# Two softmaxes of each item moved ahead of ScalarE's PSUM copies: a fused top-k attention and GELU MLP on one core

## The chip, the cores and the metric

The kernel runs on one core of a Trainium2 chip. The metric is the device time of one execution in microseconds (us). Five engines work side by side, each through its own list of instructions in order, and they wait for each other through semaphores: TensorE (PE; PEld is its weight load), VectorE (DVE), ScalarE (ACT), GpSimd (POOL) and SyncE (SP), which here only issues DMA transfers. Matrix products land in PSUM, where each named buffer ("bank") must be copied out before it can be written again.

## The reference

```python
scores = scale * np.matmul(q, k.transpose(0, 1, 3, 2))        # q, k, v: (8, 8, 576, 64)
kth = np.partition(scores, -top_k, axis=-1)[..., -top_k:-top_k + 1]   # top_k = 32
scores = np.where(scores >= kth, scores, -1000000000.0)
attn = np.exp(scores - np.max(scores, axis=-1, keepdims=True))
attn = attn / (np.sum(attn, axis=-1, keepdims=True) + 1e-09)
x = np.matmul(attn, v)              # -> (4608, 512), heads side by side
h = x @ w_in                        # (512, 2048)
g = 0.5 * h * (1.0 + erf(h / sqrt(2)))
return g @ w_out                    # (2048, 512)
```

Everything is float32.

## The kernel before

**Items and slots.** Attention is cut into 144 *items*. An item is 128 query rows of a pair of heads of one batch, so it has two score rows of 576 keys per partition (e = 0 and 1). A batch has 18 items: 16 main ones and two *last* ones (they hold the rows 512 to 575 of two pairs; `t == NM` in the code). Even batches have their last items at the end, odd batches at the start, so that four last items stand together: 52 to 55, 88 to 91, 124 to 127 (and 16 to 19 near the start). The loop at line 1174 runs over *slots* n = 0 to 147. In slot n different items are at different stages; the code writes each engine's instructions in the order in which that engine will take them:

- `scores(n + 2)`, and in even slots `scores(n + 3)` too: PE multiplies queries by keys (L406; L421 for a last item), ACT copies the result out of PSUM (L414, L425). Last items get their scores in slots of their own, odd ones included (items 53 and 55 in slots 51 and 53).
- `attend(n - 3)`: for an odd item PE makes `o` from the finished probabilities `pt` and the values (L727; L738 for last items), and `copy_x()` has ACT copy it into `xT` (L732, L744). Last items are attended later (`mids`, `even_last`): 52 in slot 56, 53 in slot 57, 54 and 55 in slot 59.
- `mlp(...)`: pieces of the MLP for tokens that are done, on PE. In even slots these are products with `w_in` (L790 into `h_ps`), in odd slots first the last such piece, then products with `w_out` (L944 into `seven`, L946 into `y_ps`). In odd slots `run_gelus()` (L806) follows the last `h_ps` piece, and ACT copies `seven` out (L962, L965).
- `transposes(n - 2)`: probabilities turned over for `attend`, by PE in odd slots (`tails`: `tp_t` L371 or L385 and L647, copied by L379 or L390 and L650; `both`: `tp` L661, copied by L676). For even items DVE transposes blocks (L595) and SP writes them to DRAM and reads them back (`write_p` L605, `read_p` L615); there only the small `t_ps` is left for PE (L371, copied by L379).
- `softmax(n - 1, e)` on ACT: `select` (L536, a Prelu with slope 2^100 that drives all scores below the k-th far down, needs `neg`) and then the exponential (L548, needs `bias`, and adds the row up into `den`; a short read of the accumulator follows).
- `top_k(n)` on DVE: four rounds of eight maxima and their replacement (L502, L505). Its last act is `inverse(n - 1)`, the reciprocal of `den` (L523). Then POOL makes `neg` and `bias` (`threshold(n)`, L516, L517), multiplies item n - 1 by the reciprocal (`normalise`, L571) and adds halves of later rows (`sum_up`, L466; `smaller`, L474). `add_small(n - 1)` (L529) stands on POOL behind `smaller(n + 1)` and before `threshold(n)`, and the reciprocal waits for it.

So there is a ring from slot to slot: end of top-k on DVE, threshold on POOL, two softmaxes on ACT, `add_small` on POOL, reciprocal on DVE at the end of the next top-k.

**PSUM.** From slot 13 on (`few[0]`, n > START + 2 with START = 10) the small results `o`, `seven`, `t_ps` and `tp_t` share one bank, tag "z": each needs the copy of the one before. `tp` and one of the two score tiles share the pair "pr", the other score tile and `h_ps` the pair "l1".

**ACT's order before,** in slots from 13 on: scores' copies; `copy_x`; in odd slots the gelus; the copy of `seven`; softmax(n - 1, 0); the copies of `tails` and `both` (or of `t_ps`); softmax(n - 1, 1); then in odd slots the remaining copies. The gelus and the exponentials need different function tables, so ACT loads a table (1.28 us) before the gelus and again before the first exponential that follows.

Of the kernel before, what the change touches and what calls it, by code (L numbers as in the profile page):

```python
# [14 lines left out]
def kernel(  # L15
# [83 lines left out]
    def issue_soon():  # L99
        while soon:  # L100
            soon.pop()()
# [140 lines left out]
    def waits(u):  # L242

        return u == ORDER[-1]
# [3 lines left out]
    def weights_add(u):  # L248
        if u in words:
            w, _, _, d = parts(u)  # L250
            nc.gpsimd.tensor_tensor(d, d, w.bitcast(i32), op=ALU.add)
        made.add(u)
# [22 lines left out]
    few = [False]  # L275
# [75 lines left out]
    def row(i, e):  # L351
        return S_of[i][:, e * S : (e + 1) * S]
# [178 lines left out]
    def select(i, e):  # L531

        if i < 0 or i >= N:
            return
        st, s = stat_of[i], row(i, e)
        nc.scalar.activation(s, s, func=AF.Prelu, bias=st["neg"][:, e : e + 1], scale=1.0, alpha=STEEP)  # L536
        selected.add((i, e))
# [3 lines left out]
    def softmax(i, e):  # L541

        if i < 0 or i >= N:
            return
        st, s = stat_of[i], row(i, e)
        if (i, e) not in selected:
            select(i, e)
        nc.scalar.activation(  # L548
            s, s, func=AF.Exp, bias=st["bias"][:, e : e + 1], scale=1.0,
            accum_out=st["den"][:, e : e + 1],  # L550
        )
# [23 lines left out]
    def squared(i):  # L575

        if not SINGLE.stop - 2 < i < N - 2:
            return False
        return items[i][1] == NM or (i % 2 == 0 and i % RINGS != 12)

    def delayed(i):

        return squared(i) and items[i][1] == NM
# [23 lines left out]
    def read_p(i):  # L607

        if squared(i):
            d = turned.pop(i)  # L610
            if i % 2 == 0:
                pt_now[0] = pt_tile()
            cols = slice(i % 2 * P, (i % 2 + 1) * P)
            for k in range(P // SQ):
                nc.sync.dma_start(  # L615
                    out=pt_now[0][k * SQ : (k + 1) * SQ, :, cols], in_=d[:, :, k, :]
                )
# [70 lines left out]
    def closes(i):  # L688

        if not few[0] or i < 0 or i >= N:  # L690
            return False
        pair, t = items[i]
        return t < NM and t % 2 == 1 and pair % NP == NP - 1

    def copy_x():
        while copies:
            copies.pop()()
# [369 lines left out]
    def run_gelus():  # L1067
        while waiting:
            gelus(waiting.pop(0))
            if eager[0]:  # L1070
                run_small(9)

    def run_small(room):

        while summing:
            sums(summing.pop(0))
            room -= 4
        while small and room > 0:
            n, f = small.pop(0)
            f()  # L1080
            room -= n
# [11 lines left out]
    def mlp(n):  # L1093
        for _ in range(n):
            if done[0] >= len(pieces) or pieces[done[0]][0] > ready[0] or left[0] == 0:
                return
            pieces[done[0]][1]()
            done[0] += 1
            left[0] -= 1
            if eager[0]:  # L1100
                run_gelus()
                run_small(9)
# [8 lines left out]
    def room_in(n):  # L1111

        x = n - START - 1
        if x < 1:
            return 4
        if x >= len(sizes):
            return 0
        return sizes[x] + (1 if x % 2 == 0 else -1) + 2 * (bare(n) - bare(n + 1))
# [55 lines left out]
    for n in range(ahead):  # L1174

        held[0] = n < N and squared(n - 2)
        mid = [i for i in (n - 5, n - 4) if delayed(i) and n % 2 and (i % 2 or i in starts)]
        even_last = delayed(n - 4) and n % 2 == 0 and n - 4 not in starts
        if not mid and not even_last:
            read_p(n - 3)  # L1180

        def mids():
            attend(mid.pop(0))
            if not mid:
                copy_x()
                read_p(n - 3)
                issue_soon()
        left[0] = room_in(n)
        few[0] = n > START + 2
        eager[0] = n > N  # L1190
        left[0] += closes(n - 3) - closes(n - 2)
        if not waits(unit_in(n)):
            weights_add(unit_in(n))
        if n > 0:
            larger(n + 1)
        for piece in squares_in.pop(n, []):
            piece()
        if n == 1:

            for e in range(2):  # L1200
                select(0, e)
            for e in range(2):
                softmax(0, e)
        two = few[0] and n % 2 == 0 and n + 3 < N and items[n + 3][1] < NM
        scores(n + 2, two)
        if two:
            scores(n + 3)
        if even_last:
            product = attend(n - 4)
            issue_soon()  # L1210
            read_p(n - 3)
        else:
            product = not delayed(n - 3) and attend(n - 3)
        if len(mid) == 2:
            mids()
        late = n > START
        if n != 1 and n < START:

            for e in range(2):
                select(n - 1, e)  # L1220
            softmax(n - 1, 0)
        copy_x()
        if n == START:

            for e in range(2):
                select(n - 1, e)
            softmax(n - 1, 0)
        if waits(unit_in(n)):
            weights_size(unit_in(n))
            weights_add(unit_in(n))  # L1230
        mlp(1)
        if closes(n - 3):
            ready[0] = n_tok[0]
        if few[0] and n % 2:
            run_gelus()
        tr = transposes(n - 2)
        if product and n > START and done[0] < len(pieces) and pieces[done[0]][0] > ready[0]:

            for piece in tr[:1]:
                piece(n + 2 if few[0] else None)  # L1240
            tr, ready[0] = tr[1:], n_tok[0]
        if not few[0] and n > START:
            softmax(n - 1, 0)
        mlp(1)
        if n != 1 and not late:
            softmax(n - 1, 1)
        if few[0]:
            softmax(n - 1, 0)
            if n % 2:
                mlp(ODD)  # L1250
                if mid:
                    mids()
        mlp(1)
        prep = prep_in.pop(n, [])
        if n == 0:
            weights_size(unit_in(1))
            keep_busy(14, ident)
        if n == START + 1:

            for piece in prep:  # L1260
                piece(None)
            prep = []
        if len(prep) > 1 and len(tr) == 3:
            tr, prep = tr[:1] + prep[:1] + tr[1:], prep[1:]
        now = tr[:-1]
        if few[0]:
            now, tr, prep = tr + prep[:1], [], prep[1:]
        for x, piece in enumerate(now):
            piece(n + 2 if few[0] else None)
            ready[0] = n_tok[0]  # L1270
            if few[0] and x == 2:
                break
            mlp(1)
        ready[0] = n_tok[0]
        if late:
            softmax(n - 1, 1)
        if n > 0:
            smaller(n + 1)
        add_small(n - 1)
        for piece in tr[-1:] + prep:  # L1280
            piece(None)
            mlp(1)
        if n < START:

            keep_busy(4 if n == 0 else 8 if product else 14 if n < 5 else 18, ident)

        run_gelus()
        mlp(left[0])
        run_gelus()
        if n < N:  # L1290
            top_k(n, lambda: inverse(n - 1), lambda: square_p(n - 2))
            write_p(n - 2)
            flush()
            if n == 0:
                larger(1)
        else:
            inverse(n - 1)
        threshold(n)
        if n == 0:
            smaller(1)  # L1300
        normalise(n - 1)
        sum_up(n + 2)
        if n in sums_in:
            weight_sums(sums_in[n])
        run_small(6)

        if n > 0 and not waits(unit_in(n + 1)):
            weights_size(unit_in(n + 1))
        run_stores()
        if n == N:  # L1310
            run_stores()
        for m in (n + 1, n + 2):

            if m > 2 and waits(unit_in(m)) == (m == n + 1):
                load_weights(m)
        if n < NP:
            load("v", n)
        if n == 5:
            nc.vector.memset(flat["k"][0][TL:, 0:TL], 0.0)
            load("q", SQUARES)  # L1320
            load("k", SQUARES)
# [38 lines left out]
```

## Time and profile before

| | |
|---|---|
| median of 3 runs | 1477.53 us (1476.33 to 1479.15) |
| the profiled execution | 1479.29 us, of which span 1477.5 us |
| instructions | 26521 |
| TensorE's granted clock | 0.999 |
| ACT in the whole span | 1082.8 us busy (73%) |
| POOL | 1142.0 us (77%) |
| L536 select | 288, mean 788 ns |
| L548 exponential | 288, mean 782 ns, and 288 reads of 194 ns |
| table loads for L806 and for L548 | 68 and 67, 1283 ns each |

In the timelines a row has the start in us, the length in us, the engine, the line in the code, the operation, the tiles as out<-in, shapes, how many instructions were merged into the row, and in brackets how long the engine stood idle before it and what ended that. Rows of merged PE instructions end with the last one's modelled end. In the list of waits a row has who waited for whom, the sum in us, how many times, and the longest. In the table by stretches the busy time of each engine follows the stretch's bounds and length.

### The profile page before, as it was taken

Reading aid. Unit: us, or ns where it says so; the run is one execution under the profiler, and the core shown is the slowest. Engines: PE = TensorE matmul, PEld = TensorE weight load, DVE = VectorE, ACT = ScalarE, POOL = GpSimd, SP = SyncE. Lnnn points to the kernel's source line nnn. Section 1 sums busy time; section 2 is a strip of 40 time slices with the busy share of each in tenths; the row PEclk is TensorE's granted clock in tenths of the full one; section 3 lists DMA queues with packets and bytes.
Section 4 is the critical chain, followed back from the end, with each engine's and each line's share of the span. In section 5 each row is a group of like instructions: output and inputs, shape, how many; then the busy total and the mean of one; then the engine's idle time right before and its main releaser. Section 6 shows DMA issues by size and latency. Waiting matters only on the chain. (4 is left out here: it accounts for less than half of the span.)

```text
span 1477.5 us, 26521 instructions
## 1 busy us (share of the span) xinstructions
PE 1449.7 (98%) x8693; PEld 1134.6 (77%) x8693; DVE 1307.8 (89%) x3331; ACT 1082.8 (73%) x1902; POOL 1142.0 (77%) x1290
## 2 busy tenths in 40 slices
PE   8999999999999998999999999999999999999999
PEld 6776677887777776888777777787777777787787
DVE  7999899999999999899999999899999999898701
ACT  7999877877777686777777777677777777677620
POOL 6877567878898888777898978787788888887632
PEclk9999999999999999999999999999999999999999
DMA  7425210045435356345534347344543435523300
GB/s 198 144 86 129 78 47 1 24 92 103 93 71 91 67 107 129 65 95 112 102 81 78 74 74 151 76 92 96 99 101 73 89 63 97 125 61 73 68 15 15
DMA packets 544713, 127.04 MB, mean 86 GB/s; under 512 B 466464, under 2 KB 536128, under 8 KB 544576
## 3 DMA queue, kind: packets, MB, share of 16 engines
q1 hardware_dynamic: 543312, 124.93, 39.8%
q8 instruction: 69, 1.13, 0.3%
q14 instruction: 68, 0.56, 0.1%
q10 hardware_dynamic: 1200, 0.39, 0.1%
q0 software_dynamic: 64, 0.03, 0.0%
HBM read 80.47 MB, written 44.83 MB: 85 GB/s over the span
## 5 line engine op out<-in xcount | busy, mean ns | idle before, releaser
L790 PE MATMUL h_ps<-xT,w_in_sb 128*128 128x256 f32 (+1 forms) x2560 | 534.1, 361 | 0.0
L790 PEld LDWEIGHTS h_ps<-xT,w_in_sb 128*128 128x128 f32 x2560 | 437.5, 190 | 73.3 <-issue 25.2
L502 DVE MAX8 top<-lists 128x8 f32<-128x576 f32 (+1 forms) x792 | 475.5, 639 | 0.0
L505 DVE MATCH_REPLACE8 lists<-top,lists 128x288 f32<-128x288 f32 (+1 forms) x528 | 307.6, 588 | 0.0
L571 POOL TENSOR_TENSOR s<-s,stat 128x1152 f32<-128x1152 f32 x135 | 286.1, 2119 | 0.3 <-DVE stat L523 0.3
L536 ACT ACTIVATE s<-s,stat 128x576 f32<-128x576 f32 x288 | 224.7, 788 | 16.6 <-POOL stat L516 16.4
L548 ACT ACTIVATE s<-s,stat 128x576 f32<-128x576 f32 x288 | 224.6, 782 | 11.3 <-POOL lists L466 0.7
L529 POOL TENSOR_SCALAR stat<-stat 128x2 f32<-128x2 f32 x144 | 31.6, 219 | 210.4 <-ACT s L548 183.8
L474 POOL TENSOR_TENSOR lists<-lists 128x576 int32<-128x576 int32 x132 | 186.4, 1412 | 4.0
L466 POOL TENSOR_TENSOR lists<-s 128x576 int32<-128x576 int32 x133 | 188.0, 1413 | 0.0
L727 PE MATMUL o<-pt,raw_v 128*64 128x256 f32 x1280 | 152.9, 384 | 4.3 <-DMA pt<-turned 2.4
L806 ACT ACTIVATE g<-h_ps 128x512 f32<-128x512 f32 x144 | 78.2, 594 | 107.0 <-PE h_ps L790 106.8
L727 PEld LDWEIGHTS o<-pt,raw_v 128*64 128x64 f32 x1280 | 87.9, 136 | 88.3 <-issue 43.1
L946 PE MATMUL y_ps<-w_out_sb,sum 128*128 128x256 f32 x472 | 140.8, 380 | 0.0
L414 ACT ACTIVATE s<-s_ps 128x1024 f32<-128x1024 f32 x127 | 124.9, 1031 | 9.2 <-PE s_ps L406 8.8
L406 PE MATMUL s_ps<-kt,qm 64*128 64x512 f32 x512 | 129.4, 618 | 0.8 <-ACT s L412 0.8
L676 ACT COPY pt<-tp 128x1024 f32<-128x1024 f32 x73 | 74.4, 1019 | 56.2 <-PE tp L661 56.1
L505 DVE MATCH_REPLACE8 lists<-first,lists 128x288 f32<-128x288 f32 x264 | 114.2, 438 | 0.0
L946 PE MATMUL y_ps<-w_out_sb,g 128*128 128x256 f32 x480 | 113.4, 379 | 0.0
L523 DVE RECIPROCAL stat<-stat 128x2 f32<-128x2 f32 x144 | 22.9, 159 | 95.2 <-POOL stat L529 94.4
L502 DVE MAX8 first<-lists 128x8 f32<-128x288 f32 x268 | 106.5, 436 | 0.0
L441 DVE TENSOR_TENSOR lists<-s 128x576 f32<-128x576 f32 x133 | 101.1, 760 | 0.0
(162 smaller groups left out, 2483.3 us busy)
## 6 DMA issues: line engine op xcount, KB each, us to landing
turned<-s SPq DMA_DIRECT2D x240, 144.0 KB, 3.5
pt<-turned SPq DMA_DIRECT2D x240, 144.0 KB, 3.2
raw_v<-in_v_dram SPq DMA_DIRECT2D x64, 128.0 KB, 3.0
raw_q<-in_q_dram SPq DMA_DIRECT2D x112, 72.0 KB, 2.3
raw_k<-in_k_dram SPq DMA_DIRECT2D x112, 72.0 KB, 2.4
out_dram<-y SPq DMA_DIRECT2D x30, 256.0 KB, 2.1
w_out_sb<-in_moe_w_in_dram SPq DMA_DIRECT2D x14, 511.8 KB, 4.8
w_out_sb<-in_moe_w_out_dram SPq DMA_DIRECT2D x10, 511.8 KB, 4.1
```

Of the source, the lines that this page charges most:

```text
L406: nc.tensor.matmul(s_ps[:, e], lhsT=q_t[rows, :], rhs=kt[rows, main_keys(pair)], start=True, stop=True)
L414: nc.scalar.activation(spread(s, S + TL, SM), s_ps, func=AF.Copy, scale=scale)
L466: nc.gpsimd.tensor_tensor(t[:, :, 1].bitcast(i32), a.bitcast(i32), b.bitcast(i32), op=ALU.add)
L474: nc.gpsimd.tensor_tensor(into_of(i)[:, :, 1].bitcast(i32), both, top, op=ALU.subtract)
L502: nc.vector.max(x[:, e], src[:, e])
L505: nc.vector.match_replace(dst[:, e], x[:, e], src[:, e], LOWEST)
L536: nc.scalar.activation(s, s, func=AF.Prelu, bias=st["neg"][:, e : e + 1], scale=1.0, alpha=STEEP)
L548: nc.scalar.activation(s, s, func=AF.Exp, bias=st["bias"][:, e : e + 1], scale=1.0, accum_out=st["den"][:, e : e + 1],)
L571: nc.gpsimd.tensor_tensor(s, s, wide, op=ALU.mult)
L727: nc.tensor.matmul(o[e * D : (e + 1) * D, 0:n], lhsT=vt[:, j, e, :], rhs=pt[:, e * NJ + j if j < NM else NM, :], start=(j == 0), stop=(j = ...
L790: nc.tensor.matmul(h_tile(u)[:, i, :], lhsT=w_in_sb[:, ko, f * P : (f + 1) * P], rhs=xT[:, ko, c0 : c0 + n], start=(ko == 0), stop=(ko == ...
L946: nc.tensor.matmul(acc[names][:, k], lhsT=lhsT, rhs=rhs, start=(j == 0 and k == 0), stop=(j == FT // 2 - 1 and k == 1),)
```

## The change

In slots from 13 on ACT's order is changed and nothing else; PE, DVE, POOL and SP get the same instructions in the same order.

- Odd slots: both selects stand ahead of `copy_x`, the gelus and the copy of `seven`; both exponentials stand where softmax(n - 1, 0) stood, ahead of the copies of `tails` and `both`, and ahead of a `copy_x` that `mids` calls.
- Even slots: select 0, exponential 0 and select 1 stand ahead of `copy_x`, exponential 1 right behind it.
- Nothing is left behind the copies of the turned probabilities.

```diff
         if n != 1 and n < START:
             for e in range(2):
                 select(n - 1, e)
             softmax(n - 1, 0)
+        if few[0]:
+            select(n - 1, 0)
+            if n % 2 == 0:
+                softmax(n - 1, 0)
+            select(n - 1, 1)
         copy_x()
+        if few[0] and n % 2 == 0:
+            softmax(n - 1, 1)
         if n == START:
...
         if n != 1 and not late:
             softmax(n - 1, 1)
         if few[0]:
-            softmax(n - 1, 0)
             if n % 2:
+                softmax(n - 1, 0)
+                softmax(n - 1, 1)
                 mlp(ODD)
                 if mid:
                     mids()
...
         ready[0] = n_tok[0]
-        if late:
+        if late and not few[0]:
             softmax(n - 1, 1)
```

`softmax` calls `select` only where it has not been called for that item and row.

## Prediction

> **What bounds the kernel now.** I read the engines' busy times on the profile's first part, then the stretches of 200 us, then the list of waits.
>
> ```profile
> PE 1449.7 (98%) x8693; PEld 1134.6 (77%) x8693; DVE 1307.8 (89%) x3331; ACT 1082.8 (73%) x1902; POOL 1142.0 (77%) x1290
> ...
> 1100.00:1300.00 200.00, 196.74 (x1188) 152.68 (x1186) 186.35 (x477) 145.91 (x259) 167.96 (x190) 0.99 0.44 92
> ...
> POOL stat L529 <- ACT s L548: 183.8, 71, 6.0
> ...
> DVE stat L523 <- POOL stat L529: 94.4, 91, 9.8
> ...
> PE o L738 <- DMA pt<-turned: 5.7, 3, 2.2
> ...
> PE o L727 <- DMA pt<-turned: 2.4, 2, 1.9
> ...
> ACT s L536 <- POOL stat L516: 16.4, 12, 2.7
> ```
>
> PE is the bound: 27.8 us of the span are not its own, and in a late stretch it works 196.74 of 200 us. Its list does not change, so a gain can only come out of its waits; the rows with `pt` hold 8.1 us, most of what there is in the slots that the change touches. DVE has 13.65 us of 200 to spare, and 94.4 us in all go to the reciprocal that waits for `add_small`, which waits 183.8 us for the exponentials. So earlier softmaxes let DVE and POOL run ahead of PE, but PE does not need them earlier in most slots. What matters is whether ACT, now waiting for the threshold ahead of its copies, makes PE wait.
>
> **An ordinary pair of slots**, 44 (even) and 45 (odd), from the timeline:
>
> ```profile
> 429.26 1.94 ACT L414 ACTIVATE s<-s_ps 128x1024 f32<-128x1024 f32 x2 [0.21 <-PE s_ps L406]
> ...
> 429.44 0.22 POOL L516 TENSOR_SCALAR stat<-top 128x2 f32<-128x2 f32 x1
> ...
> 432.43 0.37 ACT L732 COPY xT<-o 128x256 f32<-128x256 f32 x1 [1.23 <-PE o L727]
> ...
> 435.01 0.38 PE L371 MATMUL t_ps<-kt,qm 128*128 128x128 f32 x2
> ...
> 435.60 0.77 ACT L536 ACTIVATE s<-s,stat 128x576 f32<-128x576 f32 x1
> ...
> 436.40 0.78 ACT L548 ACTIVATE s<-s,stat 128x576 f32<-128x576 f32 x1
> ...
> 437.08 0.19 ACT L548 ACTIVATION_READ_ACCUMULATOR s<-s,stat 128x1 f32 x1
> ...
> 439.03 0.22 POOL L516 TENSOR_SCALAR stat<-top 128x2 f32<-128x2 f32 x1
> ...
> 439.75 1.09 ACT L806 ACTIVATE g<-h_ps 128x512 f32<-128x512 f32 x2 [1.18 <-PE h_ps L790]
> ...
> 440.72 0.38 ACT L965 COPY p<-seven 128x256 f32<-128x256 f32 x1
> ...
> 441.84 1.28 ACT L548 ACT_TABLE_LOAD   x1
> ...
> 443.00 0.38 PE L371 MATMUL tp_t<-kt,qm 128*128 128x128 f32 x2
> ...
> 443.13 0.78 ACT L548 ACTIVATE s<-s,stat 128x576 f32<-128x576 f32 x1
> ...
> 447.67 0.19 ACT L548 ACTIVATION_READ_ACCUMULATOR s<-s,stat 128x1 f32 x1
> ```
>
> A select costs 0.80 (435.60 to 436.40), an exponential with its read 0.87 (436.40 to 437.27).
>
> *Even slot.* The scores' copy ends at 431.20; `neg` was there at 429.66. Select, exponential, select take 2.47, where ACT now idles 1.23 for PE. `copy_x` then ends at 431.20 + 2.47 + 0.37 = 434.04 instead of 432.80. The next user of bank z is `t_ps` at 435.01. The 1.24 us lie inside a slack of 2.21: cost 0. Without that cover it would cost 1.24 per pair of slots.
>
> *Odd slot.* `seven`'s copy ends at 441.10, the next user of z, `tp_t`, starts at 443.00: slack 1.90. If `neg` is early, the two selects (1.60) lie in the idle time before the gelus, and only the order changes: behind `seven`'s copy (next start 440.97) come the table 1.28 and two exponentials 1.74, so both softmaxes are done at 444.0 and not 447.86, and the copy of `tp_t` begins about where it did. If `neg` is late, everything hangs behind it: from `neg` to the end of `seven`'s copy it is 1.60 + 1.28 + 0.97 (gelus to L965's start) + 0.38 = 4.2. With `neg` at 439.25 that gives 443.45, 0.45 too late for PE.
>
> So the cost depends on the *lead*: how much earlier than in this trace the threshold comes, measured against PE. It has time to grow, since the reciprocals lose their waits: up to 3.9 here (447.86 less 444.0). Ordinary odd slots need 0.5. The worst ordinary one is slot 43, where `neg` comes behind the gelus:
>
> ```profile
> 420.26 1.08 ACT L806 ACTIVATE g<-h_ps 128x512 f32<-128x512 f32 x2 [1.18 <-PE h_ps L790]
> ...
> 421.30 0.79 POOL L516 TENSOR_SCALAR stat<-top 128x2 f32<-128x2 f32 x1 [0.56 <-DVE stat L523]
> ...
> 423.51 0.38 PE L371 MATMUL tp_t<-kt,qm 128*128 128x128 f32 x2
> ...
> 424.36 0.33 PE L647 MATMUL tp_t<-ident,s 128*128 128x128 f32 x1 [0.47 <-POOL s L571]
> ```
>
> Here 422.09 + 4.2 = 426.3 against 423.51: 2.8 lost with no lead, 0 with 2.8 or more. Both ends stay for the range; I take 0, because the lead of 3.9 is the nearer row. POOL's L571 then comes earlier too, which saves PE's 0.47. The slot comes once more in each of two later batches; taken alike, 3 x 0.47: **-1.4**.
>
> **Where ACT is already late.** In slot 13 ACT's rows stand end to end from the scores' copy on, and `tp`'s copy gates the scores' bank "pr":
>
> ```profile
> 128.21 1.02 ACT L676 COPY pt<-tp 128x1024 f32<-128x1024 f32 x1
> ...
> 129.84 1.09 PE L421 MATMUL s_ps<-kt 64*64 64x512 f32 x8
> ```
>
> One more select and exponential stand ahead of that copy (1.67), so it ends at 130.9: PE loses 1.1. In slot 14 `copy_x` comes too late as well, but against a PE that is already 1.1 later: **+1.2** for both.
>
> Slots 51 and 53 (87, 89, 123, 125 alike) carry a last item's scores, whose copy comes just ahead of the gelus:
>
> ```profile
> 496.75 1.02 ACT L425 ACTIVATE s<-s_ps 128x1024 f32<-128x1024 f32 x1 [1.05 <-PE s_ps L421]
> ...
> 499.07 1.08 ACT L806 ACTIVATE g<-h_ps 128x512 f32<-128x512 f32 x2
> ...
> 500.05 0.38 ACT L965 COPY p<-seven 128x256 f32<-128x256 f32 x1
> ...
> 501.13 0.45 PE L385 MATMUL tp_t<-kt 128*64 128x64 f32 x8
> ```
>
> L425 ends at 497.77, the load takes 1.28, and the gelus start at 499.07: no idle time is left, so the two selects push them by 1.60 however early `neg` is. `seven`'s copy ends at 502.03, `tp_t` wanted z at 501.13: PE loses 0.9 to 1.0 in each, **+1.9** per group of last items. It also uses up the lead: the gelus' delay moves both softmaxes with them, and in slot 53 they end about where they did. Little lead (I take 0.2) is left for the next slots.
>
> Slots 56 to 59, where those last items are attended:
>
> ```profile
> 553.51 1.09 ACT L806 ACTIVATE g<-h_ps 128x512 f32<-128x512 f32 x2 [1.18 <-PE h_ps L790]
> ...
> 554.49 0.38 ACT L962 COPY y<-seven 128x256 f32<-128x256 f32 x1
> ...
> 555.73 0.22 POOL L516 TENSOR_SCALAR stat<-top 128x2 f32<-128x2 f32 x1
> ...
> 556.00 1.39 PE L738 MATMUL o<-pt,raw_v 128*64 128x64 f32 x40
> ...
> 558.10 3.15 SPq L615 DMA_DIRECT2D pt<-turned  x4
> ...
> 571.48 2.60 SPq L615 DMA_DIRECT2D pt<-turned  x4
> ...
> 576.82 1.39 PE L738 MATMUL o<-pt,raw_v 128*64 128x64 f32 x40 [1.21 <-DMA pt<-turned]
> ...
> 587.31 2.38 PE L727 MATMUL o<-pt,raw_v 128*64 128x256 f32 x20 [1.91 <-DMA pt<-turned]
> ```
>
> In slot 57 `neg` ends at 555.95; before, gelus and `seven`'s copy were over by then (554.87). Now they stand behind the selects: 555.75 + 4.2 = 559.95. `o` of item 53 wants z at 556.00, with the 1.9 already lost at 557.9: PE loses **2.0** more. I see nothing that gives it back: SP's read at 558.10 overwrites the `pt` that this `o` reads (it ends at 557.39), and by the order of the code the value loads, the write of item 55 and its read (571.48) stand behind it on SP's queue, so the transfers for which PE waits at 576.82 and 587.31 move with it. Slot 59's selects also stand ahead of the copy of item 54's `o`, and both exponentials ahead of item 55's; I price them at 0, since they fall into the waits of 1.21 and 1.91 that stay; without that cover they cost up to these 3.1. So 1.9 + 2.0 = 3.9 per group, three groups: **+11.7**.
>
> In slot 57 the table load stands between selects and gelus, where it was hidden before. Its row above, 441.84, ends at 443.12, and the exponential starts at 443.13: 1.28 is all it costs. The Trainium skill speaks against the change here: "ScalarE: Activation LUTs", section "What ACT_TABLE_LOAD costs", counts a drain of 1.38 us beside the load for every switch. By that rule the three groups would cost 4.1 us more (an estimate, three times 1.38), which gives 1491.9; the trace disagrees.
>
> *End.* Slots 141 to 144 have the ordinary lead; `o` there waits for a read of `pt` that hangs on DVE's transpose:
>
> ```profile
> 1395.74 2.38 PE L727 MATMUL o<-pt,raw_v 128*64 128x256 f32 x20 [1.22 <-ACT s L548]
> ```
>
> With the lead this wait goes: **-1.2**.
>
> Sum: 1.2 + 11.7 - 1.4 - 1.2 = **+10.3**. The profiled execution took 1479.29, its span of 1477.5 and 1.8 around it, so it would become 1489.6; it lies 1.8 above the median of the runs. Laid on that median, 1477.53: **1487.8**.
>
> **Rivals.**
>
> *No lead* (0.20). DVE's spare is 6.8%, and in even slots POOL sets the reciprocal (den behind L474), so the lead may not grow. Then slot 43 and its two likes cost 2.8 each and save nothing: 1487.8 + 8.4 + 1.4 = 1497.6. For it: slot 43's threshold was late though ACT was not. Against: DVE's 94.4 us of waits.
>
> *Absorbed* (0.14). The reads in slots 57 to 59 hang on DVE's transpose and not on `o`; then the stalls before them eat the 1.21 and 1.91: 3.9 - 3.1 = 0.8 per group. 1477.5 + 1.2 + 2.4 - 1.4 - 1.2 = 1478.5. For it: DVE's block transposes feed the same transfers. Against: the read at 558.10 starts 0.7 after `o` ends.
>
> *Faster* (0.16). The lead survives slots 51 and 53, since PE's own slip adds to it, and is 4.2 or more in slot 57 (555.95 + 4.2 less 556.00); from there on `seven`'s copy no longer delays `o`. The write and the reads behind it then come earlier too, and the 8.1 us of waits for `pt` go, while slots 51 and 53 still cost 1.9 per group: 1477.5 + 1.2 + 5.7 - 8.1 - 1.4 - 1.2 = 1473.7. For it: the lead of 3.9 in slot 45. Against: SP's chain, and the gelus' delay in slots 51 and 53.
>
> **Numbers.** Forecast 0.50 (its own range 1482 to 1493), no lead 0.20, absorbed 0.14, faster 0.16. A difference under 0.2% (3 us) can't be told from none here; so faster 0.16, same 0.14, slower 0.50 + 0.20 = 0.70. The range 1473 to 1499 takes in all four centres; what it leaves out is the outer halves of the first and the last rival, under 2 in 10. The ends of the unknown waits (0 and 2.8 in slot 43; 0 and 2.0 in slot 57; 0 and 3.1 in slot 59) lie inside, but not all upper ends at once.
>
> **What would show it.** Right: table loads stay 68 and 67; PE waits for L965 ahead of `tp_t` L385 in slots 51 and 53, about 0.9 each; PE waits about 2 for L962 ahead of L738 in slot 57; the wait of POOL L529 for ACT falls far below 183.8; ACT L536's wait for L516 grows from 16.4; PE's busy time stays 1450. Wrong: if L738's waits for `pt` vanish, or `tp_t` waits for L965 in many ordinary odd slots.

## The result, and the profile after

The changed kernel takes 1488.74 us, median of 6 runs (1487.04 to 1489.28); beside it the kernel before took 1477.09 (6 runs, 1476.33 to 1479.15). The ratio is 1.0076, 95% interval 1.0063 to 1.0089: slower, by more than the 0.2% that can be told apart.

The profiled execution of the changed kernel took 1488.54 us, its span 1486.8. That is 9.3 us more span than before. The rest of the 11.65 between the medians lies in which executions were profiled: the one of before stands 2.2 above its median, the one of after 0.2 below. So the traces can account for 9.3.

First the busy times of the engines and one late stretch of the kernel after:

```profile
PE 1453.4 (98%) x8693; PEld 1137.6 (77%) x8693; DVE 1332.1 (90%) x3331; ACT 1066.0 (72%) x1902; POOL 1138.5 (77%) x1290
```

```profile
1100.00:1300.00 200.00, 193.71 (x1169) 150.16 (x1168) 187.71 (x470) 139.73 (x254) 168.66 (x195) 0.99 0.45 91
```

PE has the same 8693 instructions in the same order, and works 3.03 us less in this stretch than before (196.74). DVE is busy for 24.3 us more in all, with the same 3331 instructions. Then the list of waits:

```profile
POOL stat L529 <- ACT s L548: 156.7, 70, 5.4
ACT s L536 <- POOL stat L516: 118.5, 45, 5.4
...
POOL sum L827 <- PE y_ps L946: 48.8, 13, 12.8
...
PE o L738 <- ACT y L962: 8.8, 3, 2.9
...
PE tp_t L385 <- ACT p L965: 3.7, 6, 0.6
```

ACT's selects now wait 118.5 us for the threshold, before 16.4. New are PE's waits for L962 and L965: these are `seven`'s copies that stand behind the selects (besides L385, L371 waits for L965 three times, 1.3 us). POOL's L827 now waits for PE nine times more (13, before 4).

PE's lists being the same, one can subtract the start of each instruction before from its start after; I call the difference *slip*. Every step in it is a place where PE lost or gained time. The steps over 0.3 us, with the first group of last items in detail (times are starts in the trace of before):

```
129.84  slot 13  L421   +0.86
423.51  slot 43  L371   +0.58    424.36  L647  -0.63
501.13  slot 51  L385   +0.69    520.92  slot 53  L385  +0.69
556.00  slot 57  L738   +3.00, then +1.56 while L738 and L946 run slower
559.19  slot 57  L371   -0.91
576.82  slot 59  L738   -0.76    579.41  L371  -0.30    587.31  L727  -0.79
(much the same in two more batches; in the last one also)
1283.18  L727  +0.92
1390.72  end  L647  -0.46        1395.74  L727  -1.29
at the end  +9.27
```

**Slots 51 and 13.** ACT and PE in the timeline of after:

```profile
129.55 1.02 ACT L676 COPY pt<-tp 128x1024 f32<-128x1024 f32 x1
...
130.62 1.09 PE L421 MATMUL s_ps<-kt 64*64 64x512 f32 x8 [0.79 <-ACT pt L676]
...
498.47 1.43 ACT L536 ACTIVATE s<-s,stat 128x576 f32<-128x576 f32 x2
...
501.21 1.09 ACT L806 ACTIVATE g<-h_ps 128x512 f32<-128x512 f32 x2
...
502.19 0.38 ACT L965 COPY p<-seven 128x256 f32<-128x256 f32 x1
...
502.62 0.45 PE L385 MATMUL tp_t<-kt 128*64 128x64 f32 x8 [0.62 <-ACT p L965]
```

The selects start with no idle time ahead of them (498.47, with the scores' copy just done), so the threshold was there. The gelus stand behind them, `seven`'s copy behind the gelus, and PE waits 0.62 for it.

**Slots 54 to 59.**

```profile
531.90 0.73 POOL L827 TENSOR_TENSOR sum<-g 128x256 f32<-128x256 f32 x1 [1.19 <-PE y_ps L946]
...
536.94 0.22 POOL L529 TENSOR_SCALAR stat<-stat 128x2 f32<-128x2 f32 x1
...
556.89 0.22 POOL L516 TENSOR_SCALAR stat<-top 128x2 f32<-128x2 f32 x1
557.14 1.44 ACT L536 ACTIVATE s<-s,stat 128x576 f32<-128x576 f32 x2 [5.37 <-POOL stat L516]
558.60 1.28 ACT L806 ACT_TABLE_LOAD   x1
559.90 1.08 ACT L806 ACTIVATE g<-h_ps 128x512 f32<-128x512 f32 x2
560.87 0.38 ACT L962 COPY y<-seven 128x256 f32<-128x256 f32 x1
561.30 2.34 PE L738 MATMUL o<-pt,raw_v 128*64 128x64 f32 x40 [2.93 <-ACT y L962]
...
563.68 2.57 SPq L615 DMA_DIRECT2D pt<-turned  x4
...
576.51 2.60 SPq L615 DMA_DIRECT2D pt<-turned  x4
...
581.91 1.39 PE L738 MATMUL o<-pt,raw_v 128*64 128x64 f32 x40 [0.45 <-issue]
...
591.28 2.38 PE L727 MATMUL o<-pt,raw_v 128*64 128x256 f32 x20 [1.12 <-DMA pt<-turned]
```

In slot 57 ACT idles 5.37 us for the threshold (`neg` at 557.11) and then makes selects, table, gelus and the copy one behind the other while PE stands for 2.93. SP's read of `pt` starts at 563.68, right behind `o` (561.30 + 2.34 = 563.64), as it did before (558.10, `o` over at 557.39). And `o` itself takes 2.34 where it took 1.39. The stretch behind it says why; the third number from the end is the granted clock:

```profile
561.50:564.80 3.30, 3.30 (x43) 3.00 (x42) 3.30 (x8) 2.83 (x6) 3.22 (x6) 0.50 0.02 5
```

The trace has three such pieces of 3.41 us at half clock, one behind each of the three long waits for L962. The trace of before has one too, at 1273.89, behind PE's wait of 2.20 for `pt` ahead of the L738 at 1273.51.

### The profile page after: what moved, and what is told of

It reads as the page before. It is cut to its first block, busy times and chain, and to the rows that moved or that the text cites. A ratio compares the mean times of both kernels' runs of the same rounds, so it can differ in the third digit from the quotient of the medians.

```text
span 1486.8 us, 26641 instructions
## 1 busy us (share of the span) xinstructions
PE 1453.4 (98%) x8693; PEld 1137.6 (77%) x8693; DVE 1332.1 (90%) x3331; ACT 1066.0 (72%) x1902; POOL 1138.5 (77%) x1290
## 3 DMA queue, kind: packets, MB, share of 16 engines
q8 instruction: 69, 1.13, 0.3%
## 4 chain that ended last, share of the span: by engine, by line
PE 69%; POOL 10%; ACT 5%; DVE 3%; issue 2%; DMA 2%; SPq 1%; DVEq 0%; POOLq 0%; ACTq 0%
PE h_ps L790 26%; PE y_ps L946 15%; PE o L727 8%; PE s_ps L406 5%; PE tp L661 4%; PE seven L944 2%; PE y_ps L908 2%; PE y_ps L911 2%; POOL s L571 2%; POOL lists L474 2%; PE y_ps L890 1%; ACT s L536 1%; ACT L806 1%; PE s_ps L421 1%; POOL lists L466 1%
## 5 line engine op out<-in xcount | busy, mean ns | idle before, releaser
L536 ACT ACTIVATE s<-s,stat 128x576 f32<-128x576 f32 x288 | 214.5, 774 | 118.5 <-POOL stat L516 118.5
L571 POOL TENSOR_TENSOR s<-s,stat 128x1152 f32<-128x1152 f32 x135 | 285.4, 2114 | 0.3 <-DVE stat L523 0.3
L548 ACT ACTIVATE s<-s,stat 128x576 f32<-128x576 f32 x288 | 223.2, 778 | 6.5
L466 POOL TENSOR_TENSOR lists<-s 128x576 int32<-128x576 int32 x133 | 195.1, 1467 | 0.0
L529 POOL TENSOR_SCALAR stat<-stat 128x2 f32<-128x2 f32 x144 | 31.4, 218 | 163.1 <-ACT s L548 156.7
L727 PE MATMUL o<-pt,raw_v 128*64 128x256 f32 x1280 | 153.0, 384 | 3.0 <-DMA pt<-turned 2.3
L727 PEld LDWEIGHTS o<-pt,raw_v 128*64 128x64 f32 x1280 | 87.9, 136 | 86.9 <-issue 42.2
L946 PE MATMUL y_ps<-w_out_sb,sum 128*128 128x256 f32 x472 | 141.1, 381 | 0.0
L441 DVE TENSOR_TENSOR lists<-s 128x576 f32<-128x576 f32 x133 | 125.0, 941 | 10.8 <-ACT s L379 8.1
L946 PE MATMUL y_ps<-w_out_sb,g 128*128 128x256 f32 x480 | 113.4, 379 | 0.0
L946 PEld LDWEIGHTS y_ps<-w_out_sb,g 128*128 128x128 f32 x480 | 91.2, 190 | 12.4
```

What stands on the lines that cost most here:

```text
L466: nc.gpsimd.tensor_tensor(t[:, :, 1].bitcast(i32), a.bitcast(i32), b.bitcast(i32), op=ALU.add)
L548: nc.scalar.activation(s, s, func=AF.Exp, bias=st["bias"][:, e : e + 1], scale=1.0, accum_out=st["den"][:, e : e + 1],)
L571: nc.gpsimd.tensor_tensor(s, s, wide, op=ALU.mult)
L727: nc.tensor.matmul(o[e * D : (e + 1) * D, 0:n], lhsT=vt[:, j, e, :], rhs=pt[:, e * NJ + j if j < NM else NM, :], start=(j == 0), stop=(j = ...
L946: nc.tensor.matmul(acc[names][:, k], lhsT=lhsT, rhs=rhs, start=(j == 0 and k == 0), stop=(j == FT // 2 - 1 and k == 1),)
```

## The experiments

Each kernel was compared, in five rounds, with the kernel before on the same chip; the ratios are to that. Diffs are against the changed kernel unless told otherwise. The slip was taken against the profile of the kernel before, as above.

### The two halves of the change

Even slots alone:

```diff
-        if few[0]:
+        if few[0] and n % 2 == 0:
             select(n - 1, 0)
...
         if few[0]:
+            softmax(n - 1, 0) if n % 2 else None
             if n % 2:
-                softmax(n - 1, 0)
-                softmax(n - 1, 1)
                 mlp(ODD)
...
-        if late and not few[0]:
+        if late and (n % 2 or not few[0]):
             softmax(n - 1, 1)
```

> Only the even slots are changed; odd slots keep the order of before. Theory (the loss comes from the selects ahead of the gelus in odd slots): copy_x is later by about 1.2 us but inside its slack of 2.2, so 1475 to 1479 us, no waits of PE for L965 or L962, the clock as before. Rival (the later copy_x in even slots costs a part of the loss): 1481 us or more.

1480.91 against 1478.52, ratio 1.0019 (1.0010 to 1.0027), between the two expectations. The profiled execution is the fastest of the eleven (1478.93), and its PE ends 0.34 earlier than in the trace of before, so this trace can't account for the 0.19%. The one clear loss in it stands in slot 14:

```profile
137.08 0.45 PE L385 MATMUL tp_t<-kt 128*64 128x64 f32 x8 [0.84 <-ACT xT L732]
```

This is the `copy_x` that the prediction named for slot 14; nothing comes at slots 51 to 57 beyond 0.23.

Odd slots alone:

```diff
-        if few[0]:
+        if few[0] and n % 2:
             select(n - 1, 0)
-            if n % 2 == 0:
-                softmax(n - 1, 0)
             select(n - 1, 1)
         copy_x()
-        if few[0] and n % 2 == 0:
-            softmax(n - 1, 1)
...
         if few[0]:
+            softmax(n - 1, 0)
             if n % 2:
-                softmax(n - 1, 0)
                 softmax(n - 1, 1)
...
-        if late and not few[0]:
+        if late and not (few[0] and n % 2):
             softmax(n - 1, 1)
```

> Only the odd slots are changed; even slots keep the order of before. Theory: nearly all of the loss, 1485 to 1490 us, with waits of PE for L962 ahead of L738 of about 3 us in three places and for L965 in slots 51 and 53 and their likes. Rival (even slots cost a part): 1481 to 1484 us.

1495.5, ratio 1.0117 (1.0101 to 1.0132): worse than the whole change, and outside what either theory gave. The halves do not add up (0.19% and 1.17%, together 0.76%). The slip has the steps of the whole change, larger ones in slot 43 (+1.20) and new ones: +0.97 and +0.93 in the pair "pr" at 151 and 173, +0.69, +0.69 and +0.56 in slots 23, 25 and 27, and +1.03 at a `seven` in slot 59. So the even half costs 0.2% when it stands alone and takes more than that away from the odd half's cost. Slot 43 shows how. Here `neg` ends at 426.46, 4.37 later than before, and PE comes 5.94 later: a lead of 1.6, 1.2 short of the 2.8 that the prediction worked out, and 1.20 is the loss. In the whole change the lead there is 2.2 and the loss 0.58. So the even slots' earlier softmaxes give the odd slots' thresholds some lead.

The waits of slot 57 are here as long as in the whole change, without a slower `o`. Two of the three, at 919 and 1271:

```profile
919.29 1.39 PE L738 MATMUL o<-pt,raw_v 128*64 128x64 f32 x40 [2.97 <-ACT y L962]
...
1270.92 1.39 PE L738 MATMUL o<-pt,raw_v 128*64 128x64 f32 x40 [2.97 <-ACT y L962]
```

### Selects behind the gelus

The whole change, but in odd slots the selects stand with their exponentials, behind the gelus and `seven`'s copy:

```diff
-        if few[0]:
+        if few[0] and n % 2 == 0:
             select(n - 1, 0)
```

> The whole change, but in odd slots the two selects stand behind the gelus and behind the copy of seven, still ahead of the copies of the turned probabilities. Theory: bank z is free as early as before, so no wait of PE for L965 or L962, no half clock behind such a wait, and 1473 to 1479 us. Rival (the loss comes from the exponentials ahead of the copies of tails and both, or from copy_x in even slots): 1483 us or more.

1482.72, ratio 1.0029 (1.0018 to 1.0041): more than the theory's 1473 to 1479, and just under the rival's 1483. No wait of PE for L962 or L965 is left in the list. So the selects ahead of the gelus make these waits, and moving them behind took 0.47% of the 0.76%. What stays is the other half of the edit, both exponentials ahead of `tp`'s copy. In slot 53:

```profile
524.22 0.78 ACT L548 ACTIVATE s<-s,stat 128x576 f32<-128x576 f32 x1
...
525.78 0.78 ACT L548 ACTIVATE s<-s,stat 128x576 f32<-128x576 f32 x1
...
526.86 1.02 ACT L676 COPY pt<-tp 128x1024 f32<-128x1024 f32 x1
...
527.94 1.13 PE L406 MATMUL s_ps<-kt,qm 64*128 64x512 f32 x4 [0.68 <-ACT pt L676]
```

The copy gates "pr", as it does in slot 13 (+1.07 here): slot 51 loses 0.95, slot 53 0.84.

### The slots of last items as before

The change in all slots but 13 and the odd ones 15, 17, 51, 53, 57, 59 and their likes in the other batches:

```diff
+        ex = n > START + 2 and n % 2 and (n == START + 3 or len(mid) > 0 or (n + 2 < N and items[n + 2][1] == NM))
...
-        if few[0]:
+        if few[0] and not ex:
             select(n - 1, 0)
...
                 softmax(n - 1, 0)
-                softmax(n - 1, 1)
+                if not ex:
+                    softmax(n - 1, 1)
                 mlp(ODD)
...
-        if late and not few[0]:
+        if late and (not few[0] or ex):
             softmax(n - 1, 1)
```

> The change in all slots but 13 and the odd ones that carry a last item's scores or attend a last item (15, 17, 51, 53, 57, 59 and their likes), which keep the order of before. Theory (ordinary odd slots cost nothing and the loss sits in the groups of last items): a ratio of 0.999 to 1.003, no wait for L962, the wait of 0.6 in slot 43 stays and is paid by the wait for L571. Rival (selects ahead of gelus cost in all odd slots, and the places move): 1.005 or more.

1480.38, ratio 1.0012 (1.0003 to 1.0021), end slip +1.2. Five sixths of the loss are gone with these slots, which places it where the prediction put it. In slot 43 the step stays (+0.56, -0.63).

Both edits together (selects behind the gelus, and these slots as before):

> As sel_behind (selects of odd slots behind the gelus and the copy of seven), and slots 13, 15, 17, 51, 53, 57, 59 and their likes keep the order of before, so that tp's copy no longer stands behind both exponentials there (it cost 0.95 and 0.84 in slots 51 and 53 of sel_behind and 1.07 in slot 13). Theory: against sel_behind (1.0029) it wins 1.1 + 3 x 1.8 = 6.5 us and ends at 0.997 to 1.000 of the kernel before. Rival (the even slots' change costs by itself, 1.0019 alone): 1.001 to 1.003.

1478.45, ratio 1.0004 (0.9995 to 1.0013). That decides for neither expectation (0.997 to 1.000, and 1.001 to 1.003). No loss and no gain can be measured: the end's -1.0 us and slot 43's -0.63 stand against +0.89 in slot 14. No version that I ran beats the kernel before.

### The half clock

26 products of the identity, whose result nobody reads, ahead of `o` in slot 57 and its likes, so that PE does not stand still:

```diff
+        one = len(mid) == 1
...
                 if mid:
+                    if one:
+                        spare = pair_tile("spare")
+                        for _ in range(26):
+                            nc.tensor.matmul(spare[:, 0, 0:P], lhsT=ident, rhs=ident, start=True, stop=True)
                     mids()
```

> The changed kernel with 26 small products of the identity into a free pair of banks ahead of the product o of item 53 (and of 89 and 125), where PE now waits about 3 us for the copy of seven; their result is not used. Theory (the wait of 3 us makes the clock fall to a half for 3.4 us, which costs PE some 1.4 us in each of three places): the clock stays at 1 there and the time falls by 3 to 4.5 us, to 1484 to 1486. Rival (the half clock costs nothing, since PE waits for the reads of pt behind it anyway): 1488 to 1490 us.

1496.34, ratio 1.0120 (1.0106 to 1.0133). The size was wrong:

```profile
558.28 5.97 PE L1264 MATMUL spare<-ident 128*128 128x128 f32 x52
564.18 1.39 PE L738 MATMUL o<-pt,raw_v 128*64 128x64 f32 x40
```

The filling lasted 5.97 us, twice the wait, and held `o` up by 2.88. It shows two things all the same. With PE busy the clock stays at 1.0 and `o` takes 1.39 again. And a delay of `o` in slot 57 is not given back here: `o` starts 2.88 later than in the changed kernel and ends 1.93 later, which in three places is 5.8 us, and the ratio is 0.44% or 6.5 us higher. Then with 12 products:

> As warm57, with 12 small products in place of 26: these took 5.97 us there, over twice the wait that they were to fill; 12 should take some 2.8 and end before the copy of seven does. Theory (the half clock behind the wait costs): o of item 53 starts when it does in the changed kernel, the clock stays at 1, and against the changed kernel (1.0076 of the one before) it wins 0.9 us or more in each of three places: a ratio of 1.0047 to 1.0060. Rival (the later waits for pt swallow it): 1.0070 to 1.0080.

```profile
558.79 2.84 PE L1264 MATMUL spare<-ident 128*128 128x128 f32 x24
561.88 1.39 PE L738 MATMUL o<-pt,raw_v 128*64 128x64 f32 x40 [0.25 <-ACT y L962]
...
564.97 0.49 PE L371 MATMUL t_ps<-kt,qm 128*128 128x128 f32 x2 [0.64 <-ACT xT L744]
```

1488.08, ratio 1.0066 (1.0054 to 1.0079), beside 1.0076 (1.0063 to 1.0089) of the change itself. No half clock is left in the profile, and L738 and the L946 behind it are some 1.5 us faster at each place, but then `t_ps` waits 0.64 for ACT's L744, and later waits grow too. Of three times 1.5, 4.5 us (0.30%), about 0.1% came back, less than the intervals tell apart: most of the half clock falls into waits that PE has otherwise.

### What takes the lead away

In slot 54 the sums L827 to L830 make `add_small` late, because L827 waits 1.19 for PE to have read the only `sum` tile. First I moved these sums behind `add_small` of the next even slot:

```diff
-    def run_small(room):
+    def run_small(room, hold=False):
...
-        while summing:
+        while summing and not hold:
...
         add_small(n - 1)
+        if few[0] and n % 2 == 0:
+            while summing:
+                sums(summing.pop(0))
...
-        run_small(6)
+        run_small(6, few[0] and n % 2 and n < N)
```

> The changed kernel, with POOL's four sums (L827 to L830) moved behind add_small of the following even slot. They stand ahead of smaller and add_small in the changed kernel and wait there for PE to finish with the one sum buffer (nine waits, 11.3 us, among them 2.31 in slot 38 and 1.19 in slot 54). Theory (these waits take the lead away): neg of item 56 comes at least 1.2 us earlier, PE's wait for L962 falls from 2.9 to 1.8 or less, no half clock behind it, and the ratio falls from 1.0076 to 1.003 to 1.006. Rival (DVE's own work caps the lead): the wait stays at 2.5 to 3 and the ratio at 1.007 to 1.009.

1508.33, ratio 1.0204 (1.0190 to 1.0218). It makes a wait of its own and so says nothing on the question. In slot 57, POOL and PE:

```profile
562.42 0.72 POOL L829 TENSOR_TENSOR g<-g 128x256 f32<-128x256 f32 x1
...
563.19 2.07 PE L944 MATMUL seven<-w_sum,g 128*128 128x256 f32 x4 [2.65 <-POOL g L829]
```

`seven` reads the part of `g` that L829 writes, so late sums stop PE itself.

The second try takes the wait away and leaves POOL's work and place as they are: the products read `w_sum` where they read `sum`, so nobody reads the tile that POOL fills, and L827 no longer waits for PE. (Its waits near the end stay, now for ACT's gelus: four, 31.7 us.)

```diff
-        t = sums_of[u][:, x]
+        t = w_sum[:, j, :, 0:P]
```

> The changed kernel, except that TensorE's products L946 read a part of w_sum where they read POOL's tile sum; POOL forms the same sums, but nobody reads the tile, so L827 no longer waits for TensorE (48.8 us in 13 waits in the changed kernel, of them 11.3 us in nine waits that the kernel before did not have). That part of the result is not the reference's. Theory (the single sum tile takes the lead away): the thresholds of items 54 to 56 come at least 1.2 us earlier against TensorE, L738's wait for L962 falls from 8.8 us in 3 waits to under 5.4 in all, and the ratio to the kernel before is 1.002 to 1.005. Rival (DVE's and POOL's own work caps the lead): L962's waits stay at 7.5 us or more in all and the ratio is 1.006 to 1.009. In between, both have a share.

The same edit in the kernel before:

> The kernel before with the same edit alone: L946 reads w_sum in place of sum, so that the edit's own effect is known. That part of the result is not the reference's. Both theories: L827's 31.9 us of waits in 4 lie near the start and the end, TensorE does not wait for POOL's sums in the slots of the change, so the ratio is 0.998 to 1.001. Should it fall below that, the ratio of the other kernel has to be read against this one.

In the changed kernel: 1482.44, ratio 1.0030 (1.0018 to 1.0041), where the change has 1.0076. In the kernel before: 1478.88, ratio 1.0005 (0.9996 to 1.0014), so the edit itself does nothing there. The waits for `sum` thus make some 0.46 of the 0.76% of the loss, with a part for the half clocks: this trace has one behind the three waits for L962, at 561.27, where the changed kernel has three. The steps in the slip:

```
129.84  slot 13  L421  +0.86
424.36  slot 43  L647  -0.63      (no loss at L371)
501.13, 520.92   L385  +0.69 each
556.00  slot 57  L738  +1.82      (+1.82 and +2.49 in the two later batches)
559.19  L371  -0.64    576.82  L738  -1.28    587.31  L727  -1.45
at the end  +2.65
```

And the timeline around the thresholds of slots 43 and 57:

```profile
419.06 0.22 POOL L516 TENSOR_SCALAR stat<-top 128x2 f32<-128x2 f32 x1 [0.55 <-DVE stat L523]
...
530.32 0.74 POOL L827 TENSOR_TENSOR sum<-g 128x256 f32<-128x256 f32 x1
...
555.35 0.22 POOL L516 TENSOR_SCALAR stat<-top 128x2 f32<-128x2 f32 x1
...
559.76 1.39 PE L738 MATMUL o<-pt,raw_v 128*64 128x64 f32 x40 [1.75 <-ACT y L962]
```

`neg` for slot 57 is there at 555.57, 1.54 earlier than in the changed kernel (557.11), and 1.19 earlier against PE, which has slipped 1.95 there and not 2.30. The ratio lies in the theory's range (1.002 to 1.005), but L962's waits fell from 8.8 to 5.9 us only, which is neither theory's bound (5.4 and 7.5). The rest of the wait comes from the selects standing ahead of the gelus with too little lead, as the prediction had it: 2.33 where 4.15 are needed leaves the 1.82.

## Why the prediction was right

It gave 1487.8 with the range 1473 to 1499; the result is 1488.74. The place and the mechanism were right, and the terms were off in both directions, so that the sum is better than its parts. That it came within 1 us is luck: what was missed at slot 57, the half clock and what is given back happen to cancel.

| term | predicted | slip in the trace |
|---|---|---|
| slots 13 and 14 | +1.2 | +0.86 |
| slot 43 and likes | -1.4 | 0.0 (+0.58, -0.63; +0.58, -0.62; +0.59, -0.49) |
| slots 51, 53 and likes | +5.7 | +4.1 (6 x 0.69) |
| slot 57 and likes, L738 | +6.0 | +9.0 (3 x 3.00) |
| half clock | none | +4.5 (1.44 to 1.56 each) |
| given back in slots 57 to 59 | none | -7.5 (what the other rows leave) |
| end | -1.2 | -1.75 |
| sum | +10.3 | +9.3 |

**Slots 13 and 14.** Right in place. With `tp`'s copy late, slot 14's `copy_x` cost nothing beside it, as the prediction's "already later" said; alone (even slots only) it costs 0.84. The term was 0.3 too large.

**Slot 43: "the lead of 3.9 is the nearer row".** This step failed. `neg` ended at 422.09 before. After, the rows read:

```profile
376.34 0.73 POOL L827 TENSOR_TENSOR sum<-g 128x256 f32<-128x256 f32 x1 [2.31 <-PE y_ps L946]
...
420.46 0.22 POOL L516 TENSOR_SCALAR stat<-top 128x2 f32<-128x2 f32 x1 [0.57 <-DVE stat L523]
...
424.87 0.49 PE L371 MATMUL tp_t<-kt,qm 128*128 128x128 f32 x2 [0.42 <-ACT p L965]
```

It now ended at 420.68, 1.41 earlier, with PE 0.78 later: a lead of 2.2, where the prediction had worked out that 2.8 are needed. PE lost the 0.6 that are missing. With the wait for `sum` taken away `neg` ends at 419.28, 2.81 earlier, with PE 1.13 later (L371 at 424.64): the lead is 3.9 and nothing is lost. So the reasoning on what ACT gains was sound, and what it left out is that POOL, when it runs ahead, meets the single `sum` tile that PE still reads. In slot 38 L827 waits 2.31 for it (376.34): the reciprocal, in slot 37 still 2.7 us earlier than before, is 0.65 earlier there (2.3 and 2.2 without the wait). The tile is not the only thing that takes lead: the reciprocal is 3.2 earlier in slot 32 and 1.6 in slot 33, and this loss is as large without the waits for `sum`. There DVE's L441 waits 0.72 for ACT's L379 and then takes 2.20 in place of 0.76 (323.00; the last section has the reason).

**Slots 51 and 53** lose 0.69 and not 0.95, for the stated reason: the gelus of slot 51 come 1.34 later against PE, and not 1.60, since the two selects take 1.43 one behind the other (498.47). PE did wait for L965 ahead of L385, in six places.

**Slot 57.** `neg` was to be 0.2 earlier than before and came 1.16 later (557.11 against 555.95); from `neg` to the end of the copy it took 4.14 (predicted 4.2), and PE had slipped 2.3 by then, not 1.9. So 1.36 - 0.4 = 1.0 more than the 2.0 of the forecast. Without the waits for `sum`, `neg` comes 0.38 earlier than before and PE loses 1.82: this is the prediction's case. Again the missing piece was the `sum` tile.

**"I see nothing that gives it back"** was wrong. SP's chain is as described, since the reads of `pt` moved with `o` (563.68 and 576.51, before 558.10 and 571.48). But `t_ps`, which follows `o` in bank z, waited less for L744 (-0.91), and the waits of 1.21 and 1.91 at the two later `o` shrank to 0.45 and 1.12, since the transfers moved by 5.0 and 4.3 and PE by more. In all some 2.5 us come back per group. That is about the share that the rival "absorbed" gave (3.1), for another reason than it named. In the third group 1.6 of it is the half clock that the kernel before has at 1273.89 and the changed kernel has not; 0.92 is lost again at the L727 behind.

**The half clock** was not foreseen. It costs 1.5 at each place and, by the run with 12 products, about 0.1% of the time, less than the intervals tell apart, because most of it is given back.

**End.** The wait ahead of L727 at 1395.74 is gone (-1.29), as predicted, and L647 saves 0.46 besides.

**What would show it.** L536's wait for L516 grew (16.4 to 118.5), L962 and L965 appear where they were expected, and the table loads stay 68 and 67, of 1283 ns each. The drain of 1.38 us per switch does not show here either: load 558.60 + 1.28 ends at 559.88, the gelus start at 559.90. One sign was wrong: L529's wait for ACT stays at 156.7. Taking POOL's other wait away makes it 166.2, so POOL, when it is early, waits there for the exponentials; in odd slots, which hold 138.8 of the 156.7, these still stand behind gelus that wait for PE. Of the signs against the forecast, L738's waits for `pt` did not vanish, but fell from 5.7 us to 2.2 and the 0.45 of 581.91.

Of the rivals, "no lead" was ruled out by 2.2 us of lead in slot 43; "faster" needed 4.2 us of it in slot 57, where PE's 2.3 us of slip and `neg`'s 1.16 leave 1.1.

## What to carry to other kernels

An engine that takes its instructions in order holds up every PSUM copy behind a wait: before a step that waits for another engine is moved ahead of such copies, work out how early its input must be, and in which slots there is no idle time left to cover its own length. Lead is not only made by the engine that is relieved: the first single-buffered tile that ties the faster engines to the bound one (here `sum`) can take it away, so look for such tiles in the code, since a wait for them need not be in the list yet. A loss with waits behind it on the same engine is partly given back; price those waits as cover.

## What was unexpected in the hardware

**PE's clock.** Half the clock for 3.41 us followed waits of 2.92 to 2.94 us in all three places in the changed kernel, whose mean clock was 0.995 to 0.997 in all of its six runs. Waits of the same length (2.97 and 2.98) in the kernel with the odd slots alone were followed by none; its clock was 0.998 to 1.0. The Trainium skill, "TensorE: Matmul & The Clock Gate", section "Part 1: The HAM clock gate", has the activity counted in free-running windows of 3413 ns, and the clock halved after one idle window: the length of the pieces agrees. So does their place: in the changed kernel they start at 561.41, 912.98 and 1264.55, which are 103 times 3.413 apart.

A wait of 2.93 us is shorter than such a window, and the traces show what decides: how much of the wait falls into one window. Counted back from the last piece of half clock in each trace, a window ends at 561.41 in the changed kernel, and the wait up to 561.30 lies in it whole. In the kernel with the odd slots alone one ends at 565.96, and cuts the wait up to 567.18 into 1.76 and 1.22. Over the twelve traces (without their first 30 us and the end) PE stood idle for 2.02 us or more within one window nine times, and half the clock followed each time, once in the kernel before (2.20). Of 13 windows with 1.68 to 1.91 us of idle time three were followed by it; no window with less was. So the length of a wait alone doesn't tell, and a small shift of the whole program against the windows can bring such a piece or take it away.

**DVE behind POOL.** DVE's 24.3 us of added busy time are one line, L441 (`larger`, a maximum of two halves): its 133 instructions take 941 ns in the mean, before 760. A case from before, then the same slot after:

```profile
624.66 0.76 DVE L441 TENSOR_TENSOR lists<-s 128x576 f32<-128x576 f32 x1
...
624.81 0.67 POOL L517 TENSOR_TENSOR stat<-top,first 128x2 f32<-128x2 f32 x1
625.44 2.10 POOL L571 TENSOR_TENSOR s<-s,stat 128x1152 f32<-128x1152 f32 x1
```

```profile
624.92 0.20 POOL L517 TENSOR_TENSOR stat<-top,first 128x2 f32<-128x2 f32 x1
625.07 2.11 POOL L571 TENSOR_TENSOR s<-s,stat 128x1152 f32<-128x1152 f32 x1
...
625.10 2.70 DVE L441 TENSOR_TENSOR lists<-s 128x576 f32<-128x576 f32 x1 [0.23 <-ACT s L379]
```

Before, L441 starts first and POOL's small L517 takes 0.67 in place of 0.20. After, L441 waits 0.23 for ACT's L379, which now stands behind both exponentials; L571 starts 0.03 ahead of it, and L441 ends 0.62 after L571, where it takes 0.76 alone. 14 of the 133 are over 1.3 us long, all beside an L571; before there was none. This agrees with the Trainium skill, "SBUF — State Buffer", section "SBUF: two separate sides": a DVE instruction with two inputs and a GpSimd one share a pair of ports, and who starts first has it to the end. In the first group none of them lies in slots 50 to 57. The first of them, at 323.00, takes half of the lead that there was in slot 32; what they cost in the whole was not tried.
